# Rotary attention and two MLPs in one program: the first phase's side work given out in steps, SP and GpSimd in source order

## The chip, the cores and the metric

One core of one Trainium2 chip runs the whole program. The metric is device microseconds of one execution. TensorE is called PE here, VectorE DVE, ScalarE ACT, GpSimd POOL and SyncE SP; a load of PE's weights is PEld.

## The reference

```python
# q, k, v: (4, 8, 576, 64); x: (2304, 512); both MLPs 512 -> 2048 -> 512
q_rot, k_rot = rotate(q), rotate(k)          # rotary position embedding
scores = q_rot @ k_rot.T / sqrt(64)
attn = exp(scores - max(scores)); attn = attn / (sum(attn) + 1e-9)
x = (attn @ v), heads side by side           # (2304, 512)
h = x @ moe_w_in                             # first MLP
g = where(h >= 1, h, where(h <= -1, 0, (h + 1)**2 / 4))
x = g @ moe_w_out
h = x @ moe2_w_in                            # second MLP
g = s * relu(h)**2 + b
return g @ moe2_w_out
```

The first MLP's weights arrive as float64, everything else as float32.

## The kernel before

Every float32 operand of a product is split into a high part that PE multiplies in one pass and a low part, the rest; a product is then three passes (high by high, high by low, low by high), in the scores by stacking both parts over the 128 partitions.

**The first phase** is attention, with a part of the first MLP beside it. There are 16 pairs of heads (4 batches of 4 pairs). A pair has 9 units (`UNITS`), each 128 rows of scores against 576 keys, so there are 144 units. For unit n the loop at the end of the phase calls, in the order "qltaf":

- q: `qk`: 4 matmuls of 288 columns (8 in the third unit of a pair) into `sc`; on DVE the row maximum `nm` (L301); on ACT the exponential `p` (L304), with its row sums.
- l: `do_load`: the side work for the next pair (below), and every 4th or 5th unit `convert`.
- t: `tmain` and `trem` of unit n-2: PE transposes `p` into `tp` and `tr`, ACT copies the high part (`pth`, `ptr`), DVE subtracts for the low part (`ptl`).
- a: `av` of unit n-4, after every second unit: the product with v, and its sum `u` on DVE; after a pair's last unit `finish_pair` scales `u` and stores it to the DRAM array `xd` with three DMAs.
- f: `run_fill`: pieces of the first MLP on finished batches (`beside`): 12 matmuls into `h` or `y` per piece.

The side work for the next pair is the rotation and its splits: POOL multiplies q by the table, 4 instructions, and adds the halves, 2; ACT makes the high part `qin`, DVE the low part (L245). For k POOL makes the low part too (`rope_pair`, L234 to L252). Then SP stores the parts into the stacks `qs`, `kh` and `kz` with 10 DMAs (`stack`). v is split by ACT and POOL (`vs`). `convert` turns one half of a 128-row slice of float64 weights into its two float32 parts: a load `wraw`, ACT L124, DVE L125 to L128, ACT L129, POOL 4 instructions on L87 (`wm` twice, `w` twice). There are 16 such halves in the first phase. `split_x` loads a piece of `xd` as `xs` in four DMAs and splits it on ACT (`xh`) and POOL (`xl`).

**What sets the order.** The program is written once; a scheduler then walks it with a timeline of its own and decides each engine's order of instructions, and with that the order in which SP issues DMAs. `tc.issue_after(ins)` only says that an instruction must stand behind `ins` on its engine. Every engine then works through its list strictly in order, and waits on semaphores.

**The later phases** (L570 on, `stage`) do the rest of both MLPs, with PE's order that of the source. Their text is the same in both kernels.

Of the kernel before, what the change touches and what calls it, by code (L numbers as in the profile page):

```python
# [23 lines left out]
P = 128  # L24
# [5 lines left out]
WB = 1  # L30
# [12 lines left out]
LEAD = 4  # L43
# [8 lines left out]
CF = None  # L52
# [9 lines left out]
def kernel(ctx, tc, qq, kk, vv, tab, ww1, ww2, s, b, out):  # L62
# [37 lines left out]
    class Slice:  # L100
# [5 lines left out]
        def half(self, stage, bufs):  # L106
            if self.made == 0:
# [3 lines left out]
            raw = stage.tile([P, HW], self.ww.dtype, tag="wraw", name="wraw", bufs=RB)  # L111
            nc.sync.dma_start(out=raw, in_=self.ww[self.f, :, k:k + HW])
            hi, lo = self.w[:, 0, k:k + HW], self.w[:, 1, k:k + HW]
            if not wide:
                split(hi, lo, raw, nc.scalar, nc.gpsimd)
                return


            top = raw.bitcast(F32).rearrange("p (n t) -> p n t", t=2)[:, :, 1]
            low = raw.bitcast(U16).rearrange("p (n t) -> p n t", t=4)[:, :, 1]  # L120
            a = stage.tile([P, HW], F32, tag="wa", name="wa", bufs=bufs)
            m = stage.tile([P, HW], F32, tag="wm", name="wm", bufs=bufs)
            au, mu = a.bitcast(U32), m.bitcast(U32)
            nc.scalar.activation(a, top, AF.Copy, scale=2.0 ** -112)  # L124
            nc.vector.tensor_scalar(out=mu, in0=au, scalar1=3, scalar2=None, op0=ALU.logical_shift_left)  # L125
            nc.vector.scalar_tensor_tensor(out=mu, in0=au, scalar=0x80000000, in1=mu, op0=ALU.bitwise_and, op1=ALU.bitwise_or)  # L126
            nc.vector.tensor_scalar(out=au, in0=mu, scalar1=0xFF800000, scalar2=None, op0=ALU.bitwise_and)  # L127
            nc.vector.scalar_tensor_tensor(out=a, in0=low, scalar=2.0 ** -36, in1=a, op0=ALU.mult, op1=ALU.mult)  # L128
            nc.scalar.copy(hi, m)  # L129
            pool_tt(out=m, in0=m, in1=hi, op=ALU.subtract)  # L130
            pool_tt(out=lo, in0=m, in1=a, op=ALU.add)

    chains = {}

    def accumulate(out_ps, terms, chain=None):

        n = len(terms)
        with ExitStack() as st:
            if chain in chains:
                st.enter_context(tc.issue_after(chains[chain]))  # L140
            for i, (l, r) in enumerate(terms):
                m = nc.tensor.matmul(out_ps, l, r, start=(i == 0), stop=(i == n - 1))  # L142
        if chain is not None:
            chains[chain] = m.ins
# [62 lines left out]

    WHOLE = [slice(0, S)]
# [24 lines left out]

    def rope_pair(i, nm, eng, lo_eng, pieces=WHOLE):  # L234

        t = qk_in.pop((nm, i))
        hi, lo = t[:, 0, :].bitcast(F32R), t[:, 1, :].bitcast(F32R)
        for c in pieces:
            tt = pool_tt if eng is nc.gpsimd else nc.vector.tensor_tensor
            tt(out=t[:, :, c], in0=t[:, :, c], in1=tab_sb[:, :, c], op=ALU.mult)  # L240
            r = t[:, 1, c]
            tt(out=r, in0=t[:, 0, c], in1=r, op=ALU.add)
# [3 lines left out]
            else:  # L246
                nc.scalar.copy(hi[:, c], r)
                pool_tt(out=lo[:, c], in0=r, in1=t[:, 0, c], op=ALU.subtract)
        parts_t[nm, i] = t
        if i > 0:  # L250
            stack(i, nm, 0)
            stack(i, nm, 1)  # L252

    def stack(i, nm, j):
        t = parts_t[nm, i][j * D:(j + 1) * D]
        if nm == "q":
            st = stacks["q", i, j] = qs_t[j][i % 2]
# [114 lines left out]

    def finish_pair(i, e, eb):

        bb, hp = divmod(i, NP)
        u = u_t.pop(i)
        rm = bank("rm")
        for t in range(4):
# [297 lines left out]
```

## Time and profile before

| | |
|---|---|
| Median of 3 runs | 1205.93 us (1204.47 to 1206.97) |
| Profiled execution: its own time | 1205.45 us |
| Profiled execution: span of its instructions | 1203.6 us |
| PE, DVE, ACT, POOL busy, share of the span | 92%, 66%, 50%, 51% |
| Mean granted clock of PE | 0.98 of full speed |
| First unit's exponential; last unit's | 20.1 us; 480.9 us |

The shares are means over stages that have different limits. The first phase ends shortly after 480.9 us; behind it PE is nearly full. The profile's parts of use here are the busy time by stretch (one row for a piece of the span), the waits (engine and line that waited, for whom, us in total, times, longest) and the instructions in order of time, where a bracket gives the idle time ahead of an instruction and what ended it.

### The profile page before, as it was taken

The numbers are of one execution on the slowest core, as the hardware profiler recorded it, in microseconds if no ns is written. First come the engines' busy times: TensorE is split into PE (matmuls) and PEld (weight loads), VectorE is DVE, ScalarE is ACT, GpSimd is POOL, SyncE is SP. The second block draws the span as 40 slices with busy tenths as digits, with TensorE's granted clock in tenths as the row PEclk, the third lists the DMA queues.
The fourth block names the chain that finished last, engine by engine and source line by source line (L and its number), as shares of the span: only waits on it lengthen the run. The fifth ranks groups of instructions, "written<-read, shape, count | busy, mean of one in ns | idle before, by whom it ended". The sixth has DMA issues, their size and how long they took to land.

```text
span 1203.6 us, 19127 instructions
## 1 busy us (share of the span) xinstructions
PE 1109.6 (92%) x6628; PEld 1030.7 (86%) x6628; DVE 792.4 (66%) x1363; ACT 604.5 (50%) x1315; POOL 608.5 (51%) x778
## 2 busy tenths in 40 slices
PE   2887788897999999999999899999999999999998
PEld 2676678786989999999999899989888889988887
DVE  4777798897688777677766768677853333434443
ACT  3776677775767676545444434343433233222221
POOL 6878787878445310466688897567541101111000
PEclk9898899998999999999999999999999999999999
DMA  8666656556344420343334454443421101312220
GB/s 227 197 170 194 186 161 186 160 169 180 107 130 139 109 70 31 110 127 118 115 122 137 149 173 133 143 132 102 131 65 63 32 33 63 94 32 68 68 62 34
DMA packets 75840, 142.09 MB, mean 118 GB/s; under 512 B 12000, under 2 KB 49376, under 8 KB 75744
## 3 DMA queue, kind: packets, MB, share of 16 engines
q1 hardware_dynamic: 75744, 140.88, 39.9%
q8 instruction: 52, 0.85, 0.3%
q14 instruction: 44, 0.36, 0.1%
HBM read 90.70 MB, written 26.54 MB: 97 GB/s over the span
## 4 chain that ended last, share of the span: by engine, by line
PE 48%; DVE 16%; POOL 14%; DMA 9%; issue 7%; ACT 6%; SPq 1%; POOLq 0%; ACTq 0%; DVEq 0%
PE hps L142 15%; PE yps L589 5%; PE yps L591 5%; PE yps L590 5%; POOL w L87 5%; POOL wm L87 4%; PE sc L142 4%; PE av L142 3%; PE y L142 3%; PE h L142 3%; DMA xs<-xd 3%; POOL xl L87 3%; PE tp L317 3%; DVE wm L126 2%; DVE nm L301 2%
## 5 line engine op out<-in xcount | busy, mean ns | idle before, releaser
L142 PE MATMUL hps<-xh,w 128*128 128x464 f32 (+5 forms) x1216 | 345.4, 349 | 3.6 <-POOL w L87 2.5
L87 POOL TENSOR_TENSOR xl<-xs,xh 128x232 fp32r<-128x232 f32 (+5 forms) x168 | 131.5, 807 | 256.5 <-ACT xh L91 256.3
L142 PEld LDWEIGHTS hps<-xh,w 128*128 128x128 f32 x1216 | 222.4, 189 | 19.2 <-POOL w L87 2.8
L589 PE MATMUL yps<-gh,w 128*128 128x464 f32 (+5 forms) x608 | 213.8, 352 | 6.9 <-ACT yo L596 5.6
L590 PE MATMUL yps<-gl,w 128*128 128x464 f32 (+5 forms) x608 | 213.1, 351 | 3.2 <-DVE gl L95 3.2
L591 PE MATMUL yps<-gh,w 128*128 128x464 f32 (+5 forms) x608 | 212.6, 350 | 0.0
L142 PE MATMUL hps<-xl,w 128*128 128x464 f32 (+5 forms) x608 | 211.9, 349 | 0.0
L87 POOL TENSOR_TENSOR wm<-wm,w 128x256 f32<-128x256 f32 x128 | 116.1, 927 | 126.0 <-DVE wa L127 66.8
L142 PE MATMUL sc<-kh,qs 128*128 128x288 f32 x320 | 103.5, 338 | 50.4 <-ACT p L304 32.3
L174 DVE TENSOR_TENSOR ar<-ar,hps 128x464 f32<-128x464 f32 (+1 forms) x80 | 50.6, 632 | 132.7 <-ACT ar L173 132.7
L301 DVE TENSOR_REDUCE nm<-sc 128x1 f32<-128x576 f32 x144 | 108.2, 752 | 40.0 <-PE sc L142 38.4
L589 PEld LDWEIGHTS yps<-gh,w 128*128 128x128 f32 x608 | 114.8, 189 | 17.8 <-ACT yo L596 8.2
L590 PEld LDWEIGHTS yps<-gl,w 128*128 128x128 f32 x608 | 114.8, 189 | 12.0 <-DVE gl L95 4.6
L591 PEld LDWEIGHTS yps<-gh,w 128*128 128x128 f32 x608 | 114.9, 189 | 7.5
L142 PEld LDWEIGHTS hps<-xl,w 128*128 128x128 f32 x608 | 114.5, 188 | 7.6
L304 ACT ACTIVATE p<-sc,nm 128x576 f32<-128x576 f32 x144 | 106.9, 745 | 19.3 <-DVE nm L301 15.3
L142 PEld LDWEIGHTS sc<-kh,qs 128*128 128x128 f32 x320 | 64.7, 202 | 59.4 <-ACT p L304 39.6
L323 DVE TENSOR_TENSOR ptl<-tp,pth 128x512 fp32r<-128x512 f32 x134 | 90.5, 683 | 25.9 <-ACT pth L319 24.7
L173 ACT ACTIVATE ar<-hps 128x464 f32<-128x464 f32 (+1 forms) x80 | 44.2, 553 | 124.8 <-PE hps L142 124.5
L87 POOL TENSOR_TENSOR w<-wm,wa 128x256 fp32r<-128x256 f32 x128 | 99.7, 797 | 0.0
L319 ACT CAST pth<-tp 128x512 fp32r<-128x512 f32 x134 | 77.7, 585 | 39.5 <-PE tp L317 38.9
L142 PE MATMUL sc<-kz,qs 128*128 128x288 f32 x320 | 95.1, 311 | 0.0
(85 smaller groups left out, 2289.5 us busy)
## 6 DMA issues: line engine op xcount, KB each, us to landing
wraw<-in_ww SPq DMA_DIRECT2D x64, 512.0 KB, 4.1
kh<-kin SPq DMA_DIRECT2D x64, 144.0 KB, 3.4
qs<-qin SPq DMA_DIRECT2D x64, 144.0 KB, 2.6
qin<-in_q SPq DMA_DIRECT2D x15, 576.0 KB, 5.3
kin<-in_k SPq DMA_DIRECT2D x15, 576.0 KB, 3.8
xs<-y1d SPq DMA_DIRECT2D x32, 232.0 KB, 2.5
xs<-xd SPq DMA_DIRECT2D x40, 144.0 KB, 2.6
yd<-ys SPq DMA_DIRECT2D x40, 144.0 KB, 2.1
```

Source lines behind the costliest of these rows:

```text
L87: nc.gpsimd.tensor_tensor(out=out[c], in0=in0[c], in1=in1[c], op=op)
L142: m = nc.tensor.matmul(out_ps, l, r, start=(i == 0), stop=(i == n - 1))
L173: nc.scalar.activation(r, ps, AF.Relu)
L174: nc.vector.tensor_tensor(out=r, in0=r, in1=ps, op=ALU.mult)
L301: nc.vector.tensor_reduce(out=nm, in_=sc[:, :, :288], axis=AX.XY, op=ALU.max, negate=True)
L304: nc.scalar.activation(p, sc[:, :, :288], AF.Exp, bias=nm, scale=1.0, accum_out=sums_t[i][:, col:col + 1])
L317: nc.tensor.transpose(v[:, c, :], p_t[i, k][:, c * P:(c + 1) * P], ident)
L319: nc.scalar.copy(hi, v)
L323: nc.vector.tensor_tensor(out=lo, in0=v, in1=hi, op=ALU.subtract)
L589: nc.tensor.matmul(acc, wh, gh, start=f == 0, stop=False)
L590: nc.tensor.matmul(acc, wh, gl, start=False, stop=False)
L591: nc.tensor.matmul(acc, wl, gh, start=False, stop=last)
```

## The change

**Source order for two engines.** The loop of the first phase runs inside `tc.manual_schedule` for SP and POOL: in it their instructions stand in the order in which the program writes them. DVE, ACT and PE are still ordered by the scheduler.

**Steps given out later.** `put(n, fn)` keeps a step for unit n; `run_later(n)` runs the kept steps directly behind unit n's scores, maximum and exponential. `behind` places each step's DVE and ACT instructions behind the newest maximum and exponential (`anchors`). For pair i+1 rotation and stores are spread over units 1 to 7 of pair i, a conversion's steps over 4 units from the one after it is called, the load of `xd` 3 units behind a finished batch and its splits 2 and 3 units behind the load, the store of `u` one unit and the store of `y` two units behind their sources. The whole rotation of one tile is now one step where the first pair's is done in halves.

**x in one load.** `split_x` loads all four pieces with one DMA, into the tile of the low parts, which is subtracted in place.

**Stores by kind.** The first pair's stores stand kh, kz, qs for both heads; before they alternated by head.

**Fill.** `run_fill` carries at most one unit of unused budget, and stops when the x it needs is not due yet; `LEAD` is gone.

The diff, cut to its core:

```diff
+        def steps(self, stage, bufs):
+            ...
+            return [load, bias, shift, high, rest, low_part]
...
+    anchors, later = {}, {}
+    def put(n, fn, *args):
+        later.setdefault(n, []).append((fn, args))
+    def behind(fn, *args):
+        with ExitStack() as st:
+            for ins in anchors.values():
+                st.enter_context(tc.issue_after(ins))
+            fn(*args)
+    def run_later(n):
+        for fn, args in later.pop(n, []):
+            behind(fn, *args)
...
-        nc.vector.tensor_reduce(out=nm, in_=sc[:, :, :288], axis=AX.XY, op=ALU.max, negate=True)
+        anchors["DVE"] = nc.vector.tensor_reduce(out=nm, in_=sc[:, :, :288], axis=AX.XY, op=ALU.max, negate=True).ins
...
-        nc.scalar.activation(p, sc[:, :, :288], AF.Exp, bias=nm, scale=1.0, accum_out=sums_t[i][:, col:col + 1])
+        anchors["ACT"] = nc.scalar.activation(p, sc[:, :, :288], AF.Exp, bias=nm, scale=1.0, accum_out=sums_t[i][:, col:col + 1]).ins
...
+        put(now + 1, u_store, i, u)
...
-    def split_x(c):
-        xh = m1.tile([P, KD, N1], F32R, tag="xh", name="xh")
-        xl = m1.tile([P, KD, N1], F32R, tag="xl", name="xl")
-        for k in range(KD):
-            xs = m2.tile([P, N1], F32, tag="xs", name="xs", bufs=1)
-            nc.sync.dma_start(out=xs, in_=xd[k, :, c * N1:(c + 1) * N1])
-            split(xh[:, k, :], xl[:, k, :], xs, nc.scalar, nc.gpsimd)
-        return xh, xl
+    def x_load(c):
+        x_t["h"] = m1.tile([P, KD, N1], F32R, tag="xh", name="xh")
+        x_t["l"] = m1.tile([P, KD, N1], F32R, tag="xl", name="xl")
+        nc.sync.dma_start(out=x_t["l"].bitcast(F32), in_=xd[:, :, c * N1:(c + 1) * N1].rearrange("k p n -> p k n"))
+    def x_split(k):
+        l = x_t["l"][:, k, :]
+        split(x_t["h"][:, k, :], l, l.bitcast(F32), nc.scalar, nc.gpsimd)
+    def split_x(c, n):
+        put(n, x_load, c)
+        for k in range(KD):
+            put(n + 2 + k // 2, x_split, k)
+        return n + 4
...
-                nc.sync.dma_start(out=yd[gi, d, :, c * N1:(c + 1) * N1], in_=y)
+                put(now + 2, y_store, gi, d, c, y)
...
+    def convert_turns(sl, n):
+        steps = sl.steps(wst, WB)
+        steps[0]()
+        for dn, step in zip((2, 2, 3, 3, 4), steps[1:]):
+            put(n + dn, step)
...
-                elif k == 1:
-                    rope_pair(i + 1, "q", nc.gpsimd, nc.vector)
-                elif k == 3:
-                    rope_pair(i + 1, "k", nc.gpsimd, nc.gpsimd)
-                elif k == 5:
-                    load_v(i + 1)
-                elif k == 7:
-                    v_pair(i + 1)
+                    for dn, fn, nm in ((1, rope_mult, "q"), (2, rope_add, "q"), (3, rope_hi, "q"), (4, rope_lo, "q"),
+                                       (3, rope_mult, "k"), (4, rope_add, "k"), (5, rope_hi, "k"), (6, rope_lo, "k")):
+                        put(n + dn, fn, i + 1, nm)
+                    put(n + 4, load_v, i + 1)
+                    put(n + 5, stack_q, i + 1)
+                    put(n + 6, stack_k, i + 1)
+                    put(n + 7, stack_z, i + 1)
+                    put(n + 6, v_hi, i + 1)
+                    put(n + 7, v_lo, i + 1)
...
-            convert()
+            convert(n + 1)
...
+        done = min(done, 1.0)
         done += budget
...
+    with tc.manual_schedule(engines={mybir.EngineType.SP, mybir.EngineType.Pool}):
+        while now < len(units) + LA or fill or later:
...
+                for o in ORDER:
+                    acts[o](now) if now < len(units) + LA or o == "f" else None
+                    if o == "q":
+                        run_later(now)
```

How the built programs stand, at three places. First ACT, from the transposed copies of the first pair on (`pth`; L319 before, L375 now; `wa` and `w` are a conversion's two ACT steps, `p` is a unit's exponential). Before, from its row 8, then the change, from its row 6:

```order
L319 COPY pth_211<-tp 128x4x128
L271 CAST vs<-vin 128x5x2x64
L304 ACTIVATE p,sums<-sc,nm 128x576
L124 ACTIVATE wa<-wraw 128x512
L319 COPY pth_211<-tp 128x4x128
L129 CAST w<-wm 128x512
L319 COPY pth_211<-tp 128x4x128
L304 ACTIVATE p,sums<-sc,nm 128x576
```

```order
L375 COPY pth_207<-tp 128x4x128 x3
L360 ACTIVATE p,sums<-sc,nm 128x576
L289 ACTIVATE qin<-qin 128x576
L389 COPY ptr_208<-tr 64x384
L360 ACTIVATE p,sums<-sc,nm 128x576
L375 CAST pth_274<-tp 128x4x128
L360 ACTIVATE p,sums<-sc,nm 128x576
L291 CAST kin<-kin 128x576
```

The conversion is gone from pair 0; its first ACT step now stands behind the exponential of pair 1's third unit. Up to the end of pair 4 ACT begins 6 conversions before and 8 now.

Second ACT where the first x is split (`xh`; L91 before, L89 now). Before, pair 1's seventh unit and on; then the change, the end of pair 4:

```order
L304 ACTIVATE p,sums<-sc,nm 128x576
L353 COPY u<-av 64x320
L91 CAST xh<-xs 128x288
L319 COPY pth_469<-tp 128x4x128
L304 ACTIVATE p,sums<-sc,nm 128x576
```

```order
L375 CAST pth_3202<-tp 128x4x128 x2
L389 CAST ptr_3204<-tr 64x256
L89 CAST xh<-xl 128x288 x2
L417 COPY u<-av 64x320
L360 ACTIVATE p,sums<-sc,nm 128x576
L89 CAST xh<-xl 128x288 x2
```

Before, one quarter of the first x is split after each of the pairs 0 to 3; now all four quarters are, a batch's four pairs being stored.

Third POOL, about pair 2 (multiplications by `tab_sb` and additions are the rotation for the next pair, `wm` and `w` a conversion, `eb` the sums of the pair before). Before, from row 43, then the change, from row 48:

```order
L87 TENSOR_TENSOR kin<-kin,tab_sb 128x2x144 x4
L87 TENSOR_TENSOR w<-wm,wa 128x256 x2
L87 TENSOR_TENSOR xl<-xs,xh 128x288
L87 TENSOR_TENSOR kin<-kin 128x288 x2
L87 TENSOR_TENSOR qin<-qin,tab_sb 128x2x144 x4
L370 COPY eb<-sume 128x512
L87 TENSOR_TENSOR kin<-kin,tab_sb 128x2x144 x4
L87 TENSOR_TENSOR qin<-qin 128x288
```

```order
L85 TENSOR_TENSOR qin<-qin,tab_sb 128x2x144 x4
L426 COPY eb<-sume 128x512
L85 TENSOR_TENSOR wm<-wm,w 128x256 x2
L85 TENSOR_TENSOR w<-wm,wa 128x256 x2
L85 TENSOR_TENSOR qin<-qin 128x288 x2
L85 TENSOR_TENSOR kin<-kin,tab_sb 128x2x144 x4
L85 TENSOR_TENSOR kin<-kin 128x288 x4
```

Before, the multiplications of k stand ahead of `eb`, up to a pair early, and the parts of a rotation are mixed with conversions. Now q, k and their low parts follow `eb` in one run, with a conversion's four instructions between, and k's low part (the last two of the x4) comes last.

On PE the counts of product matmuls per pair move by a few; behind the last pair's transposes 72 `h` and `y` matmuls are left, 48 before. On SP the last four `y` stores now stand behind eleven `xs` loads of the next phase, where five such loads stood ahead of the first of them.

## Rows read from the trace of the kernel before

**Rows 1.** Busy time by stretch; columns: PE, PEld, DVE, ACT, POOL, PEclk, DMA share, GB/s.
```profile
45.10:146.60 101.50, 79.53 (x510) 67.93 (x507) 80.55 (x137) 74.03 (x171) 80.37 (x100) 0.92 0.66 181
146.60:303.20 156.60, 131.19 (x917) 121.80 (x918) 137.62 (x246) 109.95 (x259) 125.53 (x155) 0.95 0.62 175
303.20:480.90 177.70, 172.22 (x1313) 168.36 (x1312) 135.69 (x256) 124.62 (x303) 56.88 (x75) 0.99 0.34 96
...
515.00:1203.60 688.60, 671.27 (x3529) 620.80 (x3527) 395.07 (x651) 258.16 (x500) 299.53 (x380) 1.00 0.31 95
200.00:250.00 50.00, 42.21 (x302) 39.50 (x302) 45.25 (x82) 36.37 (x88) 39.09 (x48) 0.97 0.64 181
```

**Rows 2.** Waits of PE and ACT, 45.1 to 303.2 us.
```profile
PE sc L142 <- ACT p L304: 23.7, 17, 4.7
...
ACT xh L91 <- DMA xs<-xd: 21.2, 11, 5.7
```

**Rows 3.** SP in order of time, 104 to 110 us.
```profile
104.29 0.42 SPq L386 DMA_DIRECT2D xd<-u  x1
...
109.91 0.33 SPq L396 DMA_DIRECT2D xs<-xd  x1
```

**Rows 4.** ACT in order of time, 106 to 114 us.
```profile
106.23 0.42 ACT L361 COPY u<-av 64x320 f32<-64x320 f32 x1
112.38 0.43 ACT L91 CAST xh<-xs 128x288 fp32r<-128x288 f32 x1 [5.72 <-DMA xs<-xd]
```

**Rows 5.** ACT in order of time, pair 0's first conversion.
```profile
24.93 0.74 ACT L304 ACTIVATE p<-sc,nm 128x576 f32<-128x576 f32 x1
...
27.79 0.66 ACT L124 ACTIVATE wa<-wraw 128x512 f32<-128x512 f32 x1 [2.02 <-DMA wraw<-in_ww]
...
30.66 0.62 ACT L129 CAST w<-wm 128x512 fp32r<-128x512 f32 x1 [1.73 <-DVE wm L126]
...
31.66 0.74 ACT L304 ACTIVATE p<-sc,nm 128x576 f32<-128x576 f32 x1
```

**Rows 6.** DVE groups, 45.1 to 303.2 us: busy us, mean ns.
```profile
L128 DVE SCALAR_TENSOR_TENSOR wa<-wraw,wa 128x512 f32<-128x512 uint16 x16 | 13.8, 862 | 0.2
L126 DVE SCALAR_TENSOR_TENSOR wm<-wa,wm 128x512 uint32<-128x512 uint32 x16 | 13.5, 845 | 0.2
...
L125 DVE TENSOR_SCALAR wm<-wa 128x512 uint32<-128x512 uint32 x16 | 11.6, 726 | 3.6 <-ACT wa L124 3.6
...
L127 DVE TENSOR_SCALAR wa<-wm 128x512 uint32<-128x512 uint32 x16 | 8.2, 510 | 0.2
```

**Rows 7.** POOL groups, 45.1 to 303.2 us.
```profile
L87 POOL TENSOR_TENSOR kin<-kin,tab_sb 128x288 f32<-128x288 f32 x40 | 35.4, 914 | 6.2 <-DMA kin<-in_k 3.8 <-issue 2.4
L87 POOL TENSOR_TENSOR wm<-wm,w 128x256 f32<-128x256 f32 x30 | 25.4, 865 | 19.7 <-DVE sume L368 6.9 <-DVE wa L127 6.8 <-ACT pth L319 3.6
L87 POOL TENSOR_TENSOR w<-wm,wa 128x256 fp32r<-128x256 f32 x30 | 21.6, 738 | 0.0
L87 POOL TENSOR_TENSOR kin<-kin 128x288 f32<-128x288 f32 x21 | 17.7, 854 | 0.0
```

**Rows 8.** ACT in order of time: exponentials of pair 2's first and fifth, pair 3's first unit.
```profile
69.92 0.75 ACT L304 ACTIVATE p<-sc,nm 128x576 f32<-128x576 f32 x1
...
80.53 0.74 ACT L304 ACTIVATE p<-sc,nm 128x576 f32<-128x576 f32 x1
...
90.88 0.74 ACT L304 ACTIVATE p<-sc,nm 128x576 f32<-128x576 f32 x1
```

**Rows 9.** DMA issues: count, KB each, median us to landing.
```profile
kz<-kin SPq DMA_DIRECT2D x32, 144.0 KB, 3.1
```

**Rows 10.** The conversion's tile wa, 45.1 to 303.2 us: ns shortest/median/longest.
```profile
L125 DVE TENSOR_SCALAR wm<-wa x16: 404/820/1029, 48.6 to 295.3; 128x512 uint32<-128x512 uint32 x16
```

**Rows 11.** The y copies' tile, 303.2 to 481 us: DMA to landing.
```profile
DMA to landing us min/median/max: 1.7/2.0/3.6
```

**Rows 12.** ACT in order of time behind the last pair.
```profile
497.05 0.43 ACT L91 CAST xh<-xs 128x288 fp32r<-128x288 f32 x1 [3.79 <-DMA xs<-xd]
```

More of the change, by code (lines that the diff above doesn't have):

```diff
@@ L106, in half @@
         def half(self, stage, bufs):
+            for step in self.steps(stage, bufs):
+                step()
+        def steps(self, stage, bufs):
             if self.made == 0:
@@ L133 @@
-    chains = {}
-    def accumulate(out_ps, terms, chain=None):
-        n = len(terms)
[L138 to L144, printed above, removed]
+                return [load, lambda: split(hi, lo, t["raw"], nc.scalar, nc.gpsimd)] + [lambda: None] * 4
@@ new lines, in high, with rest, low_part @@
+            def high():
+                nc.scalar.copy(hi, t["m"])
+            def rest():
+                low = t["raw"].bitcast(U16).rearrange("p (n t) -> p n t", t=4)[:, :, 1]
+                a = t["a"]
+                nc.vector.tensor_scalar(out=a.bitcast(U32), in0=t["m"].bitcast(U32), scalar1=0xFF800000, scalar2=None, op0=ALU.bitwise_and)
+                nc.vector.scalar_tensor_tensor(out=a, in0=low, scalar=2.0 ** -36, in1=a, op0=ALU.mult, op1=ALU.mult)
+            def low_part():
+                m = t["m"]
+                pool_tt(out=m, in0=m, in1=hi, op=ALU.subtract)
+                pool_tt(out=lo, in0=m, in1=t["a"], op=ALU.add)
@@ L433 @@
     load_v(0)
-    rope_pair(0, "k", nc.vector, nc.gpsimd, HALVES)
-    rope_pair(0, "q", nc.vector, nc.vector, HALVES)
-    for j in range(2):
-        stack(0, "k", j)
-        first = stack(0, "q", j)
-    v_pair(0)
+    rope_first("k")
+    rope_first("q")
+    stack_k(0)
+    stack_z(0)
+    first = stack_q(0)
+    v_hi(0)
+    v_lo(0)
     nc.sync.dma_start(out=s_sb, in_=s.to_broadcast([P, 1]))
@@ L461, in run_fill @@
             try:
-                done -= next(fill[0])
+                cost = next(fill[0])
+                if cost is None:
+                    break
+                done -= cost
             except StopIteration:
@@ L517 @@
     acts = {"q": do_qk, "l": do_load, "t": do_t, "a": do_av, "f": do_fill}
-    for n in range(len(units) + LA):
-        with ExitStack() as st:
-            if n < 36:
-                st.enter_context(tc.issue_after(first))
-            for o in ORDER:
-                acts[o](n)
-    while fill:
-        run_fill(1.0)
+    now = 0
+    with tc.manual_schedule(engines={mybir.EngineType.SP, mybir.EngineType.Pool}):
+        while now < len(units) + LA or fill or later:
+            with ExitStack() as st:
+                if now < 36:
+                    st.enter_context(tc.issue_after(first))
+                for o in ORDER:
+                    acts[o](now) if now < len(units) + LA or o == "f" else None
+                    if o == "q":
+                        run_later(now)
+            now += 1
     pa.close()
```

141 lines of the change are left out of this document (83 added, 58 removed).

## The prediction, made before the changed kernel ran

> **What bounds the kernel now.** I read the busy time by stretch first, cut at the first exponentials of pairs 0, 1, 5 and 10 at the last unit and where the next phase begins. The reader should see three regimes [rows 1]. From 515 us on PE is nearly full: 671.27 of 688.60 us. The change doesn't touch that code, so nothing is to be had there. From 303.2 to 480.9 us PE is busy 172.22 of 177.70 us; what the change could win is 5.5 us at the most. The room is ahead of that. In pairs 1 to 4 (101.5 us) no engine is full: PE 79.53, DVE 80.55, POOL 80.37, ACT 74.03. In pairs 5 to 9 (156.6 us) DVE has 137.62, PE 131.19. So 283 us, the 25 of pair 0 with them (20.1 to 45.1), go to engines that wait for each other, and the question is what they wait for.
>
> The waits say it next. PE waits 23.7 us for exponentials, to reuse its score buffers [rows 2]. So the pace is that of maximum and exponential, and I ask what stands in their way on ACT and DVE. On ACT the largest wait for something outside the units is `xh` for its load: 21.2 us in 11 waits [rows 2]. In order of time one reads like this: SP issues the store of `u` at 104.29 us, and the load `xs` of the same data only at 109.91 [rows 3]; ACT, done at 106.65, stands until 112.38, 5.72 us, with copies and exponentials queued behind `xh` [rows 4]. A second kind is a conversion ahead of its data. In pair 0 ACT waits 2.02 us for `wraw` and 1.73 us for DVE inside one conversion, and two neighbouring exponentials are 6.7 us apart, 24.93 to 31.66 [rows 5].
>
> **The change part by part.** The sum is made on the profiled execution, 1205.45 us (its span 1203.6); the median of the runs is 1205.93, 0.5 us above.
>
> *Pair 0.* No conversion is left in it. Its four DVE steps, two ACT steps and the load wait go. The gap of 6.7 us falls to a common unit: pair 2 took (90.88 - 69.92)/9 = 2.3 us for each [rows 8]. That is 4.4 us. Against it the second qs store of the first head now stands behind two more kh and one more kz; SP takes about 0.5 us for an issue (0.42 for the one in rows 3), and the first scores wait for it: 0.5 us. **Minus 4.** Bounds: 0, if pair 0 then waits for the next pair's k instead; 5.
>
> *Pairs 1 to 4.* The three `xs` waits in here go, since the load now follows the store by two units and the splits follow the load by two more; two more conversions come in (8 begun by the end of pair 4, 6 before). A conversion costs DVE 862 + 845 + 726 + 510 ns = 2.94 us [rows 6], POOL 2 x 865 + 2 x 738 = 3.2 us [rows 7]. DVE's work is then 80.55 + 5.9 = 86.4 us, POOL's 80.37 + 6.4 = 86.8. The fullest long stretch of the trace while POOL is also busy has DVE at 45.25 of 50 us, 90% [rows 1]. At that packing the stretch would take 96 us, 5.5 less. But here there is no product work to fill with and the rotation's own chain (first rival) is close behind, so I take **minus 2**. Bounds: minus 10 (DVE at 94%) and plus 7 (the rival).
>
> *Pairs 5 to 9.* Two conversions fewer: DVE's work 137.62 - 5.9 = 131.7 us; the `h` matmuls and their steps are as many as before. The other eight `xs` waits go. One DMA issue and its landing take the place of four; two units lie ahead of the first split, and I let them cover it: a unit here is 156.6/45 = 3.5 us, two are 7, and one quarter's load took 2.5 us from issue to use [rows 3, 4]. If the fourfold load took more than 7 us, ACT would wait again. At 90.5% of DVE the stretch takes 145.5 us: **minus 11**. Bounds: 0 and minus 18 (95%).
>
> *Pairs 10 to 15.* PE is full, so gains end here. A new cost: `y` has two buffers, and its store now comes two units after the copy. The third copy of a piece waits for the first one's store, which lands 2.0 us after its issue [rows 11], behind the qs, kh and kz stores on SP. ACT has 53 us free in this stretch, so most of it hides. **Plus 4**, from 0 to 12 (1 us on ACT for half of the 24 copies if it hides behind nothing).
>
> *End of the phase.* 72 matmuls instead of 48 are left behind the last transposes; the last `h` need ACT and DVE in turn, while ACT splits the next phase's x in the same list and already waits 3.79 us for a load there [rows 12]. Before, PE had cover for it. **Plus 3**, 0 to 6.
>
> The store of `u` one unit later, v's split, the merged tiles: nothing, as the first is read two units later and POOL's and ACT's counts stay the same. SP in source order: each of its waits is about one unit behind the step it waits for; what could be late is kz, the rival below.
>
> Sum: 1205.45 - 4 - 2 - 11 + 4 + 3 = **1195 us**.
>
> **The rivals.** *POOL's list becomes the bound (slower).* Now k's rotation stands behind `eb` and a conversion in strict order. Take pair 2's first exponential as zero. The conversion's POOL part waits for its last DVE step, which is placed behind the maximum of a later unit, in pair 2 of its fifth, whose exponential comes at 10.6 us [rows 8]. Add that DVE step 0.86 [rows 6], POOL's part 3.2, k's multiplication 4 x 0.914 = 3.7, addition 1.7, high part on ACT about 0.7 (as long as the exponentials, 0.74), low part 1.7, the landing of kz 3.1 [rows 9], scores and maximum some 1.5: the next pair's first exponential at 27.2 us. A pair took 101.5/4 = 25.4. So pairs 1 to 4 lose 7.3 us; if pairs 5 to 9 gain nothing for the same reason, the time is 1205.45 - 4 + 7.3 + 7 = 1216. It decides once kz lands later than two exponentials ahead of its pair. For it: POOL is already 79 to 80% busy there [rows 1]. Against: POOL runs ahead whenever its data are there, only some pairs have the conversion ahead of k, and at 2.3 us a unit, the mean of the same pair, the fifth exponential would come at 9.2 us, which takes 1.4 us off the chain.
>
> *DVE and POOL can't be packed closer (no change).* L125 takes 404 ns at best and 1029 at worst on the same shape [rows 10]. Something stretches DVE's SBUF-to-SBUF work here. If it and POOL excluded each other fully, the bound on pairs 1 to 9 would be POOL's 80.37 + 125.53 = 205.9 us [rows 1] plus DVE's conversions, 13.8 + 13.5 + 11.6 + 8.2 = 47.1 us [rows 6]. That is 253 us of 258.1, so 5 us to win at most; I take 3, and the time is 1205.45 - 4 - 3 + 7 = 1205. Against: if they stretch each other, these durations contain their own waits, and the true bound lies lower. The Trainium skill, "SBUF — State Buffer", section "Who interferes with whom", says just this: a DVE instruction with two SBUF inputs, or in a two-port mode, and a GpSimd instruction that reads SBUF lock each other out for a whole instruction. The trace agrees in kind, with the 404 and 1029 ns above; by that rule the time would be this rival's.
>
> *DVE packs to 95% and the new costs hide.* Minus 10 and minus 18 in the two stretches, minus 4 at the start: 1174 with nothing given back, some 1181 with both late costs.
>
> **How the numbers follow.** Forecast 0.56, POOL bound 0.22, no closer packing 0.13, close packing 0.09. About 0.2% (2.4 us) is what a measurement of this kernel can tell from no change. The forecast's own range, 1187 to 1204, holds a small part within that. Faster 0.56 x 0.95 + 0.09 = 0.62; within 0.2%: the rest of the forecast, 0.03, and 0.10 of the third case: 0.13; slower 0.22 + 0.03 = 0.25. The range goes from 1178, inside the close packing, to 1216, the price of the POOL bound.
>
> **What would show it.** Right: no `xh` waits of several us on ACT in pairs 1 to 9; no 6.7 us between exponentials of pair 0; the first exponential of pair 10 some 17 us earlier than 303.2, DVE about 90% busy in pairs 5 to 9; PE's wait for exponentials well below 23.7 us. For the first rival: PE waits for kz at the first scores of pairs 2 to 5, and ACT's high part of k waits for POOL. For the second: longer means on POOL and DVE than in [rows 6, 7], the stretch as long as before. The late costs would be ACT's `ys` waiting for the store of `y`, and a gap of PE near the last pair's end. I am wrong if pairs 1 to 9 are not shorter, or if the time lies outside 1178 to 1216.

## The result, and the profile of the changed kernel

The change makes the kernel slower: 1214.8 us (median of 6 runs, 1212.77 to 1220.86) against 1205.0 us for the kernel before on the same chip; the ratio is 1.0084, its 95% interval 1.006 to 1.0108. The forecast was faster, 1195 us. The profiled execution of the changed kernel took 1214.13 us (span 1212.4), 8.7 us more than before.

Busy time by stretch of the changed kernel, cut at the same exponentials as [rows 1], with pair 0 ahead; columns as there:

```profile
20.80:40.70 19.90, 17.64 (x102) 14.98 (x101) 9.43 (x15) 14.56 (x35) 7.97 (x11) 1.00 0.49 131
40.70:153.20 112.50, 84.74 (x515) 70.60 (x514) 88.32 (x153) 75.53 (x173) 80.74 (x102) 0.91 0.59 170
153.20:302.30 149.10, 127.85 (x911) 118.67 (x911) 128.25 (x230) 106.73 (x254) 110.38 (x139) 0.97 0.55 162
302.30:482.90 180.60, 171.33 (x1294) 164.85 (x1293) 138.62 (x259) 123.60 (x306) 80.26 (x105) 1.00 0.41 119
```

Pair 0 is 5.1 us shorter (19.9 against 25.0) and pairs 5 to 9 are 7.5 us shorter (149.1 against 156.6). But pairs 1 to 4 are 11.0 us longer (112.5 against 101.5), pairs 10 to 15 2.9 us longer, and from the last exponential to the end there are 729.5 us, 6.7 more than before (722.8).

The waits of PE and ACT in the changed kernel, pairs 1 to 9 (engine, line, whom for: us in total, times, longest):

```profile
ACT p L360 <- DVE nm L357: 13.9, 13, 3.2
PE sc L156 <- ACT p L360: 11.3, 13, 2.1
PE sc L156 <- DMA kz<-kin: 7.9, 5, 2.8
ACT xh L89 <- DMA xl<-xd: 5.6, 3, 3.6
```

The wait that the change is about fell: ACT's `xh` stands 5.6 us for its load where it stood 21.2 (3.6 of the 5.6 are one wait, for the first load of x at the end of pair 4), and PE's wait for exponentials fell from 23.7 to 11.3 us [rows 2]. In its place PE now waits 7.9 us for `kz`, k's low part, for which nothing waited in these pairs before. Where that stands is seen at the end of pair 3, on SP and then on PE, in order of time (start, duration; in brackets the idle time ahead and what ended it):

```profile
112.35 0.60 SPq L316 DMA_DIRECT2D kh<-kin  x1
112.99 0.58 SPq L119 DMA_DIRECT2D wraw<-in_ww  x1
113.67 1.10 SPq L321 DMA_DIRECT2D kz<-kin  x2
...
117.28 0.31 PE L156 MATMUL av<-ptr,vs 128*128 128x320 f32 x1
119.55 0.40 PE L156 MATMUL sc<-kz,qs 128*128 128x288 f32 x1 [1.96 <-DMA kz<-kin]
```

SP issues a load of weights, `wraw`, and 0.7 us later the two kz stores. PE runs dry at 117.59 us and gets kz at 119.55; the next pair's first exponential follows at 121.2, 7.5 us after the issue. Before, kz was issued 7 to 45 us ahead of its pair (pairs 1 to 10), as POOL and SP ran up to a pair ahead.

The load ahead of kz is waited for as well. ACT and DVE at the same place, and ACT at the end of pair 4:

```profile
118.64 0.66 ACT L129 ACTIVATE wa<-wraw 128x512 f32<-128x512 f32 x1 [2.30 <-DMA wraw<-in_ww]
119.33 0.43 DVE L134 TENSOR_SCALAR wm<-wa 128x512 uint32<-128x512 uint32 x1 [2.07 <-ACT wa L129]
120.32 0.76 DVE L357 TENSOR_REDUCE nm<-sc 128x1 f32<-128x576 f32 x1
...
149.79 0.76 ACT L89 CAST xh<-xl 128x288 fp32r<-128x288 f32 x2 [3.61 <-DMA xl<-xd]
```

At the end of pair 3 the maximum `nm` stands on DVE behind the conversion's step and one that follows ACT's next copy, so with kz there earlier it could hardly have started before 120.3 us. At the end of pair 4 PE stands 2.78 us for kz, until 150.68, and ACT for x until 149.79; the next pair's first exponential, at 153.24, stands behind both.

### The profile page after: what moved, and what is told of

Read it like the earlier page. It is cut to its first block, busy times and chain, and to the rows that moved or that the text cites. A ratio compares the mean times of both kernels' runs of the same rounds, so it can differ in the third digit from the quotient of the medians.

```text
span 1212.4 us, 19014 instructions
## 1 busy us (share of the span) xinstructions
PE 1113.7 (92%) x6628; PEld 1030.9 (85%) x6628; DVE 790.4 (65%) x1363; ACT 602.1 (50%) x1315; POOL 602.5 (50%) x778
## 4 chain that ended last, share of the span: by engine, by line
PE 47%; POOL 15%; DVE 15%; issue 8%; ACT 7%; DMA 6%; SPq 2%; POOLq 0%; ACTq 0%; DVEq 0%
PE hps L156 15%; PE yps L678 5%; PE yps L680 5%; PE yps L679 5%; POOL w L85 4%; POOL wm L85 4%; PE sc L156 4%; PE y L156 4%; PE h L156 3%; DMA kz<-kin 3%; PE av L156 3%; POOL xl L85 3%; DVE wm L135 2%; DVE nm L357 2%; PE tp L373 2%
## 5 line engine op out<-in xcount | busy, mean ns | idle before, releaser
L85 POOL TENSOR_TENSOR xl<-xs,xh 128x232 fp32r<-128x232 f32 (+5 forms) x140 | 106.0, 787 | 216.9 <-ACT xh L89 216.9
L156 PE MATMUL sc<-kh,qs 128*128 128x288 f32 x320 | 102.8, 336 | 37.9 <-DMA qs<-qin 18.7
L678 PEld LDWEIGHTS yps<-gh,w 128*128 128x128 f32 x608 | 115.1, 189 | 18.7 <-ACT yo L685 8.1
L360 ACT ACTIVATE p<-sc,nm 128x576 f32<-128x576 f32 x144 | 107.3, 746 | 27.5 <-DVE nm L357 24.6
L375 ACT CAST pth<-tp 128x512 fp32r<-128x512 f32 x134 | 77.8, 586 | 43.3 <-PE tp L373 42.2
```

The lines of the kernel that those rows point to most:

```text
L85: nc.gpsimd.tensor_tensor(out=out[c], in0=in0[c], in1=in1[c], op=op)
L360: anchors["ACT"] = nc.scalar.activation(p, sc[:, :, :288], AF.Exp, bias=nm, scale=1.0, accum_out=sums_t[i][:, col:col + 1]).ins
L375: nc.scalar.copy(hi, v)
L678: nc.tensor.matmul(acc, wh, gh, start=f == 0, stop=False)
```

## The experiments

Each ratio is to runs of the kernel before on the same chip, with its 95% interval; the stretches come from one profiled execution each, cut as above. "kz" is the median time from issue to landing of the kz stores between 40 and 160 us. How far a stretch repeats is seen on two kernels with the same program through pair 11: the change and e11 took 112.5 and 111.1 us for pairs 1 to 4, but 149.1 and 156.2 for pairs 5 to 9. The profiled execution of e7 is the fastest of its six, 1186.7 us against a median of 1192.7; e16, the same program through pair 13, took 99.3 and 142.6 us for these two stretches.

| run | ratio | pairs 1-4 | 5-9 | 10-15 | behind | kz |
|---|---|---|---|---|---|---|
| before | 1 | 101.5 | 156.6 | 177.7 | 722.8 | 4.6 |
| change | 1.0084 | 112.5 | 149.1 | 180.5 | 729.5 | 4.3 |
| e1 k two units earlier | 1.0414 (1.0392-1.0436) | 121.6 | 172.1 | 189.8 | 729.0 | 3.0 |
| e2 stores at once | 1.0215 (1.0188-1.0241) | 116.6 | 164.1 | 179.1 | 731.2 | 4.5 |
| e3 change, free order | 1.0125 (1.0104-1.0147) | 107.3 | 161.5 | 177.7 | 732.2 | 6.2 |
| e4 before, source order | 1.1355 (1.1332-1.1377) | 155.7 | 244.9 | 202.0 | 723.1 | 2.6 |
| e5 k one unit earlier | 1.0089 (1.0069-1.0108) | 110.2 | 152.2 | 179.3 | 731.8 | 2.7 |
| e6 before + x | 0.9975 (0.9957-0.9994) | 94.8 | 159.3 | 173.3 | 732.3 | 5.6 |
| e7 before + rotation | 0.9904 (0.9882-0.9927) | 96.1 | 142.4 | 179.6 | 722.5 | 3.0 |
| e8 before + x + conversions | 1.0019 (0.9998-1.0041) | 90.7 | 167.2 | 173.1 | 731.9 | 5.2 |
| e9 before + rotation + x | 1.0067 (1.0043-1.0092) | 106.4 | 150.5 | 176.4 | 733.1 | 5.2 |
| e10 as e9, + conversions | 1.0107 (1.0081-1.0133) | 103.7 | 160.9 | 181.1 | 730.4 | 5.2 |
| e11 change, more fill | 1.0075 (1.0046-1.0104) | 111.1 | 156.2 | 184.7 | 722.6 | 3.9 |
| e12 as e9, more fill | 1.0027 (1.001-1.0045) | 107.4 | 147.6 | 183.3 | 722.4 | 5.2 |
| e13 change, loads clear of kz | 1.0063 (1.0039-1.0087) | 105.7 | 156.2 | 182.5 | 730.4 | 2.7 |
| e14 change, two loads in the way | 1.0156 (1.0132-1.018) | 119.5 | 150.1 | 181.5 | 730.3 | 6.1 |
| e15 as e13, more fill | 1.0053 (1.0034-1.0072) | 103.1 | 155.4 | 185.0 | 722.2 | 2.7 |
| e16 as e7, more fill | 0.9923 (0.9906-0.9939) | 99.3 | 142.6 | 181.7 | 729.3 | 3.4 |
| e17 as e9, no cap | 1.0149 (1.0107-1.0192) | 103.7 | 163.9 | 186.8 | 716.0 | 4.7 |
| e18 as e13, cap early | 1.0082 (1.005-1.0115) | 103.8 | 159.4 | 188.1 | 726.4 | 2.7 |

### e1 and e5: k earlier

```diff
-(3, rope_mult, "k"), (4, rope_add, "k"), (5, rope_hi, "k"), (6, rope_lo, "k")
+(1, rope_mult, "k"), (2, rope_add, "k"), (3, rope_hi, "k"), (4, rope_lo, "k")
```

In e1 with stack_k at n + 4 and stack_z at n + 5; in e5 all these numbers are one larger.

> The changed kernel with the four rotation steps of k and its kh and kz stores two units earlier; all else as in the change. Theory A (kz comes just in time, so the next pair's first scores wait): kz is issued some 5 us earlier in each pair, PE's wait for kz in pairs 1 to 9 falls from 9.6 us to under 3, pairs 1 to 4 from 112.6 us to 103 to 108, and the time to 1204 to 1209. Theory B (DVE and POOL stretch each other and cannot be packed closer): the kz waits go, but others take their place, pairs 1 to 4 stay at 110 to 115 us, the time at 1212 to 1217. Theory C (the stores of y and the late fill at the phase's end): 1212 to 1217 as well, with the milestones behind 480 us unchanged relative to the last exponential.

> The changed kernel with the rotation steps of k and its kh and kz stores one unit earlier, so that its multiplication still stands behind eb in POOL's list (two units earlier it stood ahead of eb, and the third unit of a pair then waited for eb). Theory A (kz just in time): PE's wait for kz in pairs 1 to 9 falls from 9.6 us to under 4, pairs 1 to 4 from 112.6 us to 106 to 110, the time to 1206 to 1211. Theory E (in a strict list every place moved ahead makes something else late: conversion, eb, ACT's list): kz's waits shrink, others grow by as much, 1213 to 1225.

Two units earlier PE's wait for kz is down to 0.5 us, and the kernel is 4% slower. The waits of e1, 40 to 334 us:

```profile
PE rm L434 <- POOL eb L426: 43.0, 9, 12.4
DVE u L435 <- PE rm L434: 23.9, 5, 10.4
```

k's multiplication now stands ahead of `eb`, the finished pair's sums, in POOL's strict list, and PE stands for `eb` up to 12.4 us at a time. One unit earlier, PE waits 12.7 us for `eb` in pairs 1 to 9 and 5.7 for kz, and the time is that of the change, as theory E had it. Theory A in its simple form (kz is late, so move it) fell: the place that k leaves is taken from something that is needed as much.

### e2, e3, e4: stores at once, and the order

```diff
-put(now + 2, y_store, gi, d, c, y)
+y_store(gi, d, c, y)
-put(now + 1, u_store, i, u)
+u_store(i, u)
```

> The changed kernel with the stores of u and y written where their data are made, not one and two units later; SP still in source order. Theory C (delayed stores hold back the end of the phase): ACT's ys no longer waits for the store of y, the time from the last exponential to the end falls from 729.5 us towards 723, the time to 1207 to 1210. Theory A: the end gains at most 2 us, and SP, which now stands before each store until its data are there, issues kz no earlier or later: 1212 to 1219.

> The changed kernel without the source order: steps and their places behind maxima and exponentials kept, SP and POOL ordered by the scheduler again. Theory D (source order on SP and POOL is what makes kz late): POOL and SP run ahead, kz is issued 7 us or more ahead of its pair, pairs 1 to 4 take 101 to 105 us, the time is 1202 to 1207. Theory A in its narrow form (the steps are late, since ACT's high part of k stands behind the exponential of the sixth unit whatever the order on SP and POOL): kz is no earlier than in the change, pairs 1 to 4 take 109 to 114 us, 1211 to 1217.

> The kernel before with its first phase in source order on SP and POOL, and nothing else of the change: rotation written at units 1 and 3, stores right behind it. Theory D (source order is what costs): SP stands before each store and load until its data are there, POOL behind conversions; pairs 1 to 4 take 108 us or more, the time is 1212 or more. Theory A in its narrow form (the late steps cost, not the order): k is rotated from the fourth unit of a pair on, kz is in time, pairs 1 to 4 take 100 to 106 us, the time is 1202 to 1209.

e3 takes the line `with tc.manual_schedule(...)` out of the change; e4 puts it around the loop of the kernel before. Theory D fell in e3 and came out in e4. In e3 kz is issued 8 to 11 us ahead at the ends of pairs 1 to 4, as theory D wanted, and pairs 1 to 4 take 107.3 us; but pairs 5 to 9 take 161.5, and without source order the steps are no faster (1.0125 against 1.0084). So in the change source order is not what costs. Without the steps it costs 13.6%: e4 waits, 41 to 442 us,

```profile
PE rm L379 <- POOL eb L370: 123.3, 9, 28.7
POOL wm L87 <- DVE wa L127: 66.7, 6, 15.6
```

show POOL standing at a conversion with `eb` queued behind it. Steps placed units later are what makes such an order bearable. e2 says the same of SP: with the stores at once the ratio rises by 1.3%, most of it in pairs 5 to 9, so the delays of u and y help; the end does not get shorter (731.2 us), and theory C fell.

### e6 to e10: the parts one by one, SP and POOL free

Each is the kernel before with parts of the change's diff, the order left to the scheduler. The part on x (its fill rule with it), the rotation with its stores, and the conversions, by their calls:

```diff
-x = split_x(work[0][0])
+ready = split_x(work[0][0], now + 3)
...
-rope_pair(i + 1, "q", nc.gpsimd, nc.vector)
+for dn, fn, nm in ((1, rope_mult, "q"), (2, rope_add, "q"), (3, rope_hi, "q"), (4, rope_lo, "q"),
...
-convert()
+convert(n + 1)
```

e6 has the first, e7 the second, e8 the first and third, e9 the first and second, e10 all three.

> The kernel before with only the part on x: one load of all four pieces three units after a finished batch, splits two and three units later behind the newest maximum and exponential, the fill waiting for it; rotation, conversions, stores and SP's and POOL's free order as before. Theory A (the x part gains, the late rotation costs): no waits of ACT's xh for a load in pairs 1 to 9, pairs 5 to 9 at 145 to 150 us, the time 1194 to 1201. Rival (the x waits only covered other waits): 1203 to 1209.

> The kernel before with only the rotation, v's split and their stores given out as the change does it, behind maxima and exponentials; x, conversions, y and u stores and SP's and POOL's free order as before. Theory A (late rotation is the cost): PE waits for kz 8 us or more in pairs 1 to 9, pairs 1 to 4 at 107 to 113 us, the time 1210 to 1220. Rival (the rotation steps are harmless, conversions in POOL's list make them late): kz's waits under 3 us, 1202 to 1208.

> The kernel before with the part on x and with the conversions in steps, rotation and stores as before, free order. Theory A: as with x alone, and pair 0 free of its conversion: 1191 to 1199. Rival (conversion steps behind maxima hold up POOL's rotation): kz waits of several us, pairs 1 to 4 at 107 us or more, 1205 to 1215.

> The kernel before with the rotation given out in steps and the part on x (its fill rule with it), conversions, u and y stores and the free order as before. Theory F (rotation steps gain, and only together with the conversion's steps do they cost): pairs 1 to 4 at 90 to 98 us, last exponential at 450 to 463 us, the stretch from it to the end at 730 us or more as with x alone, so 1182 to 1194. Rival (any two parts get in each other's way): pairs 1 to 4 above 101 us, 1203 to 1215.

> As the run with rotation and x, and the conversions in steps too; only the delayed stores of u and y and the source order are then missing from the change. Theory F: pairs 1 to 4 at 104 to 112 us with PE waiting for kz 10 us or more, 1213 to 1224, as the change with SP and POOL free (1221). Rival G (the delayed stores of u and y cost, not the conversions): pairs 1 to 4 at 90 to 99 us, 1184 to 1198.

x alone (e6) gains 0.25%, less than expected: `xh` waits only 0.5 us for its load in pairs 1 to 9, but pairs 5 to 9 take 159.3 us, not 145 to 150. The conversions in steps add 0.4% both times (e8 to e6, e10 to e9; the latter two intervals overlap). They lengthen pairs 5 to 9 (167.2 and 160.9 us); pairs 1 to 4 get no longer with them (90.7 and 103.7 us). Theory F fell with e9.

e7 turned the picture round. The rotation in steps, which I had as the cost, gains 1% alone and makes the fastest kernel of all. Its stretches (pairs 1 to 4, 5 to 9) and two of its waits, pairs 1 to 9:

```profile
44.40:140.50 96.10, 78.32 (x510) 64.70 (x507) 83.89 (x147) 74.05 (x172) 80.13 (x104) 0.96 0.62 180
140.50:282.90 142.40, 125.74 (x914) 117.32 (x915) 127.61 (x227) 105.14 (x252) 107.71 (x133) 0.99 0.59 172
...
ACT xh L91 <- DMA xs<-xd: 4.8, 5, 2.1
PE sc L142 <- DMA kz<-kin: 3.8, 4, 1.5
```

With x untouched, four loads and all, the `xh` waits are down from 21.2 us to 4.8. And kz is just as late as in the change: issued 4.7 to 7.4 us ahead of its pair (pairs 1 to 9; 4.2 to 11.0 in the change). So lateness alone is not the cost, and x in one load is not needed for the gain. With rotation and x together (e9) pairs 1 to 4 take 10 us more than with rotation alone (8 us from e16 to e12). The landing times of kz, 40 to 160 us, in e7, e9 and e6, in this order:

```profile
DMA to landing us min/median/max: 2.5/3.0/5.1
...
DMA to landing us min/median/max: 3.0/5.2/6.6
...
DMA to landing us min/median/max: 2.7/5.6/6.0
```

At the median kz lands 2 us later in e9 than in e7. But only at the end of pair 4 does a load of x stand ahead of it, by 3.6 us (the first kz store lands in 4.9 us, in e7 in 2.5). At the end of pair 3 it is the load of a later pair's k, 576 KB, 0.5 us ahead (5.5 us, in e7 2.5), and at the end of pair 1 one of weights, which e7 has there too (6.5 and 5.1 us). In e6, where POOL runs up to a pair ahead, kz lands as late, but from pair 2 on it is issued 9 to 49 us ahead, PE never waits for it between 40 and 160 us, and pairs 1 to 4 take 94.8 us. So it seems to take both: a late kz, and something that holds up its landing.

### e13 and e14: loads out of kz's way, and into it

In e13 a conversion's load of weights that would fall in the sixth to eighth unit of a pair is issued in the fifth, its other steps unmoved, and the first load of x stands behind kz; in e14 two loads (units 17 and 25) are issued in units 15 and 24.

```diff
-if n > 5 and n % (CA if n < 36 else CB) == 0:
-    convert(n + 1)
+for c in CONV:
+    if early(c + 1) == n + 1:
+        convert(n + 1, c + 1)
```

Here `CONV` lists the old units, the second argument sets the other steps, and `early(n)` is `n - n % 9 + 4 if n % 9 in (5, 6, 7) else n` in e13 and `{17: 15, 25: 24}.get(n, n)` in e14.

> The changed kernel in which a conversion's load of weights that would be issued in the sixth to eighth unit of a pair is issued in the fifth, all its other steps where they were, and the first load of x is issued two units later, behind kz. Theory J (a large load issued just ahead of kz delays kz's landing): the time from the issue of kz to the next pair's first exponential falls from 7.5 to about 5 us at the end of pair 3 and from 11.0 to 5 to 6 at the end of pair 4; pairs 1 to 4 at 103 to 108 us, the time at 1205 to 1211. Rival K (what makes these pairs long is the order on ACT, DVE and POOL, not the loads): the times from issue to exponential fall little or the pairs stay at 110 to 114, 1212 to 1218.

> The changed kernel in which two loads of weights (of the third and the fifth conversion) are issued two and one units earlier, between the stores of kh and kz of pairs 2 and 3, where none stands in the change; all other steps where they were. Theory J: from issue of kz to the first exponential 7 us or more for pairs 2 and 3, 4.2 and 4.9 in the change; pairs 1 to 4 longer by 4 to 8 us, 1218 to 1223. Rival K: no difference beyond 1 us in these pairs, 1212 to 1217.

e14, end of pair 2, on SP, PE and DVE; here the change had `kh` and `kz` side by side:

```profile
91.81 0.59 SPq L316 DMA_DIRECT2D kh<-kin  x1
92.45 0.59 SPq L119 DMA_DIRECT2D wraw<-in_ww  x1
93.14 1.10 SPq L321 DMA_DIRECT2D kz<-kin  x2
...
99.09 0.40 PE L156 MATMUL sc<-kz,qs 128*128 128x288 f32 x1 [3.17 <-DMA kz<-kin]
...
99.80 1.42 DVE L357 TENSOR_REDUCE nm<-sc 128x1 f32<-128x576 f32 x2 [2.89 <-PE sc L156]
```

and kz's landing between 40 and 160 us in e13, in the change and in e14:

```profile
DMA to landing us min/median/max: 2.6/2.7/2.7
...
DMA to landing us min/median/max: 2.6/4.3/8.4
...
DMA to landing us min/median/max: 5.7/6.1/7.4
```

Boundary by boundary (ends of pairs 1, 2, 3, 4) the landing takes 2.6, 2.7, 6.0 and 7.8 us in the change, 2.6, 2.7, 2.7, 2.7 in e13 and 5.9, 6.1, 6.1, 7.1 in e14: with each load of 512 KB put ahead of kz it takes 3.3 to 3.4 us more, and with each taken away it comes back. From issue of kz to the first exponential pairs 2 and 3 go from 4.2 and 4.9 us to 9.2 and 7.5 (e14), pairs 4 and 5 from 7.5 and 11.0 to 4.5 and 4.4 (e13). Pairs 1 to 4 follow: 105.7 us in e13 (103.1 and 103.8 in e15 and e18, which place the loads alike), 112.5 in the change, 119.5 in e14. So the place of these loads sets the length of this stretch, as theory J had it. The Trainium skill, "DMA: Bandwidth & Descriptors", section "Queues, rings and completion order", gives a reason: a DMA engine takes one queue's descriptors in ring order, and the semaphore is raised only after that engine's earlier writes. The trace agrees with it, 6.0 against 2.7 us.

How much of this is kz alone is not shown. Of the ends in e14 that of pair 2, above, shows kz's landing by itself, and there it costs 2.6 us. At the end of pair 1 PE also works in another order than in the change: ten products with v, 3.05 us, stand ahead of the first product with kz, not behind it, and PE goes from them to kz without a gap. And e13 takes away more than the load ahead of kz. ACT's waits for `wraw` and `xl`, 3.4 and 3.6 us in pairs 1 to 4 of the change, go with it, and some work on the first x falls behind pair 4 (DVE is busy 85.4 us in the stretch, 88.3 in the change). In e18 kz lands within 3.6 us, and still 7.5 us pass at the end of pair 3 from its issue to the exponential.

The whole time followed up (1.0156) but only a little down: 1.0063 has an interval that overlaps the change's. e13, e15 and e18 take 155 to 159 us for pairs 5 to 9, where the first x, and with it the fill, comes two units later; whether that is why was not tried, and e11, without it, took 156.2.

### e11, e12, e15 to e18: the end of the phase

```diff
-run_fill(0.55 if n < 18 * NP + LA else 0.95)
+run_fill(0.55 if n < 18 * NP + LA else 0.95 if n < 108 else 1.05)
```

This is e11, e12 and e15; in e16 the 1.05 starts at unit 126. e17 drops `done = min(done, 1.0)`; e18 keeps it up to unit 90 only.

> The changed kernel with a budget of 1.05 pieces a unit from the thirteenth pair on, not 0.95, so that 60 product matmuls are left behind the last transposes, 12 of them h, not 72 with 24 h behind the last product with v. Theory H (the new fill rule leaves h matmuls behind the last pair, whose chain over DVE and ACT nothing covers): the stretch from the last exponential to the end falls from 729.5 to 721 to 725 us, of which part may come back before it, 1207 to 1211. Rival (the late y stores hold the end): 1213 to 1217.

> The run with rotation and x, with that budget of 1.05 from the thirteenth pair on. Theory F and H together: 1176 to 1187, that is 6 us below the run with rotation and x. Rival (pairs 10 to 15 are full, what is filled earlier lengthens them by as much): the same time as that run.

> The kernel of the run with the loads clear of kz, with a budget of 1.05 pieces a unit from the thirteenth pair on. Theory J with H: 2 to 4 us below that run, 1202 to 1208, with the stretch from the last exponential to the end at 722 to 724 us. Rival: as that run, what is won at the end being lost ahead of it.

> The kernel before with only the rotation in steps (ratio 0.990 alone), and a budget of 1.05 pieces a unit in the last two pairs, so that no h matmul is left behind the last product with v. Theory H: 1 to 3 us below rotation alone, a ratio of 0.987 to 0.990 to the kernel before. Rival (pairs 14 and 15 are full): the ratio of rotation alone, 0.990 to 0.993. If the gain of rotation alone hangs on the chip it ran on, a ratio over 0.995.

> The run with rotation and x (ratio 1.007), with unused fill budget kept, not capped at one unit, so that no product matmul of the first MLP's part is left behind the last pair. Theory H (the cap is what x brought along): the stretch from the last exponential to the end at 722 us or less, not 733, a ratio of 0.990 to 0.998. Theory J (the large load of x ahead of kz and the later fill lengthen pairs 4 to 9): the end is shorter, but pairs 1 to 9 stay at 250 us or more and the ratio above 0.999.

> The changed kernel with the loads clear of kz (ratio 1.0063), and the cap on unused budget only up to the tenth pair, so that 42 y matmuls and no h are left behind the last transposes. Theory H: the stretch from the last exponential to the end at 720 to 724 us and a ratio of 0.998 to 1.003. Rival (pairs 10 to 15 are full): 1.004 to 1.008.

Every kernel with the new fill rule unaltered has 729 to 733 us behind the last exponential. In the change PE stands there, and the granted clock falls (PE in order of time, then busy time by stretch):

```profile
509.86 0.29 PE L156 MATMUL y<-gh,w 128*128 128x288 f32 x1
511.97 0.40 PE L678 MATMUL yps<-gh,w 128*128 128x288 f32 x1 [1.83 <-ACT ys L494]
...
502.00:507.00 5.00, 5.00 (x40) 5.00 (x39) 2.11 (x6) 2.03 (x5) 2.60 (x4) 1.00 0.49 126
507.00:512.00 5.00, 3.17 (x25) 2.94 (x23) 3.30 (x8) 4.00 (x10) 1.25 (x2) 1.00 0.24 80
512.00:517.00 5.00, 5.00 (x26) 5.00 (x27) 1.14 (x3) 1.29 (x2) 1.75 (x3) 0.66 0.54 166
```

The 24 more matmuls at 5.00/40 = 0.125 us make 3.0 us, the gap 1.8, and 5 us at a granted clock of 0.66 cost 1.7: together 6.5 of the 6.7 us. With the larger budget this part falls to 722 us (e11, e12, e15), as theory H had it; but pairs 10 to 15 grow by 4.2, 6.9 and 2.5 us. What is left over is seen once: from e9 to e12 the ratio falls from 1.0067 to 1.0027, with intervals that just touch. From e13 to e15 and from the change to e11 nothing can be told. e17 and e16 bound it. Without any cap (e17) the end is 716 us, but the fill piles up in pairs 5 and 9 (38.5 and 42.8 us long) and the kernel is slower still. With no h left behind the last pair (e16) PE reaches the next phase before its x is split, the end takes 729.3 us, and the ratio is no better than e7's. e16, PE and busy time by stretch:

```profile
486.04 0.40 PE L142 MATMUL hps<-xh,w 128*128 128x288 f32 x1 [2.15 <-ACT xh L91]
...
488.30:493.30 5.00, 4.64 (x20) 4.38 (x19) 3.69 (x6) 2.45 (x6) 2.96 (x4) 0.50 0.59 168
```

So the fill rule is at most a part of why e9 is slower than e7: e12, without the long end, is still at 1.0027. e18 shortened the end to 726.4 us only and did not beat the kernel before. The versions that beat both are e7, e16 and, by 0.25%, e6.

## Why the prediction was wrong

**Pairs 1 to 4: the step that failed.** The forecast was minus 2, within minus 10 and plus 7; it came out at plus 11. Of the 18.7 us between the forecast's sum (minus 10) and the measured span (plus 8.7), 13 stand here. The step let DVE take two more conversions and be packed to 90%, less something for the rotation's chain. DVE's work came out nearly as forecast (88.3 us against 86.4), but DVE was busy 79% of the stretch: the waits for loads and stores that now come just in time were put at nothing. kz was taken for a matter of the first rival alone, whose price was plus 7.3 (its terms add up to 27.1 us, not 27.2, which makes it 6.8).

That rival named the right wait. That its time, 1216 us, is nearly the measured one is luck: it had pairs 5 to 9 unchanged and 7 us lost behind them, and measured are minus 7.5 and plus 9.6. Its reason was half of it. It put the lateness on POOL's list, with a conversion ahead of k, and took the landing at the median of 3.1 us [rows 9]. But e7 has the same lateness without conversion steps, and is fast. What I did not work out is that source order on SP also fixes which load stands just ahead of kz: at the ends of pairs 3 and 4 that is a load of weights, or of weights and x, the landing takes 6.0 and 7.8 us, and ACT stands for these loads itself. The order in which SP issues could be read ahead of the run; the page's median hid the range. Some 7 of the 11 us go when these loads are moved (e13), by kz's landing and the loads' own waits together; the runs don't part the two.

The other 4 us stay open. Pair 2 took 26.2 us against 21.0 before, and 26.5 in e13, with kz landing in 2.7 us. The number of conversions alone is not the reason: e7 begins nine by the end of pair 4, the change eight, and pairs 1 to 4 take 96.1 us in e7. Of the second rival, the locking of DVE and POOL, the sign did not come as a whole: the four DVE steps of a conversion took 2.54 us at the mean in pairs 1 to 9, 2.94 before. A small part shows in DVE's low part of q in pairs 1 to 4, in the change and in e7; the mean of the change is made of 1.2 to 1.4 us three times and 3.45 us once, in pair 4, with POOL's multiplications and additions beside it:

```profile
L297 DVE SCALAR_TENSOR_TENSOR qin<-qin 128x576 fp32r<-128x576 f32 x4 | 7.3, 1834 | 0.6 <-ACT qin L289 0.6
...
L284 DVE SCALAR_TENSOR_TENSOR qin<-qin 128x576 fp32r<-128x576 f32 x4 | 3.4, 838 | 0.0
```

**Pair 0: right.** Minus 4 was forecast; the first exponential of pair 1 comes at 40.7 instead of 45.1 us, 4.4 earlier. ACT's third and fourth exponentials, 6.7 us apart in [rows 5], now start at

```profile
24.81 0.74 ACT L360 ACTIVATE p<-sc,nm 128x576 f32<-128x576 f32 x1 [2.21 <-DVE nm L357]
...
28.75 0.75 ACT L360 ACTIVATE p<-sc,nm 128x576 f32<-128x576 f32 x1
```

They are 3.9 us apart, not the 2.3 forecast, so this gap gave 2.8 of the 4.4 us; where the rest was won was not looked into.

**Pairs 5 to 9: the mechanism right, the size uncertain.** Minus 11 was forecast, minus 7.5 measured; the same program in e11 took 156.2 us, minus 0.4. The `xh` waits did fall as forecast, from 7.4 to 2.0 us here (the trace of before has seven of them here and four in pairs 1 to 4, not eight and three). That two units cover the fourfold load held for the later loads, which landed in 4.1 to 5.0 us; the first, in pair 4, took 8.2. DVE was busy 86%, not 90.5. And e7 shows that they fall, and 14 us with them, by the rotation's steps alone.

**Pairs 10 to 15 and the end.** Plus 4 was forecast and 2.9 measured; ACT's `ys` did stand for the store of `y`, 4.0 us in two waits. For the end plus 3 was forecast, 0 to 6, and 6.7 measured. The extra matmuls alone make 3.0; the gap, which the forecast named among its signs, and the granted clock after it come on top.

**What stays open.** With the loads clear of kz the kernel is still 0.5 to 0.8% slower than before (e13, e15, e18), so they are not the whole reason. Rotation alone gives 0.990, x alone 0.9975, both 1.0067: together 1.9% worse than their product. In pairs 1 to 4 most of it stands between the issue of kz and the first exponential of pairs 2 to 5 (e9 loses 8.4 us there to e7, 7.3 of them by the landing of the first store). Why pairs 5 to 9 are 8 us longer is not settled. It is not a load of x ahead of kz: at the ends of pairs 5 and 9 that load has landed before kz is issued, and at the ends of pairs 7 and 8 the load ahead is one of weights.

## What to carry to other kernels

Before a transfer is made to come just in time, read what the same queue issues in the few microseconds ahead of it: a load of 512 KB there made two stores land 3.3 to 3.4 us later, and where the consumer was 9 us or more away (e6) PE never waited for them. See also whether that load is itself waited for. Try the parts of a change one by one: here the best part, alone, was worth 1%, and the whole was a loss. Shortening the last stretch by moving work ahead of it gains little when the stretch ahead is full.

## What the hardware showed unexpectedly

At the ends of pairs 1 to 4 of the change, e13 and e14 the two kz stores of 144 KB landed 2.6 to 2.7 us after their issue when no load stood just ahead of them, and 5.7 to 6.3 when a 512 KB load was issued 0.7 us ahead; with a load of weights and one of x ahead, 6.8 to 8.4. A gap of PE of 1.8 us was followed by a granted clock of 0.66 over the next 5 us, part of it at the lower of the two levels (1.2 of 2.4 GHz); in the kernel before the clock stayed at 1.00 there. In pairs 1 to 4 the mean granted clock was 0.96 in e7, 0.91 in the change and 0.86 in e14, but 0.90 in e13, which is 6.8 us shorter there than the change. DVE's low part of q took 0.75 us twice where POOL stood still (e7), and 1.2 to 3.45 us beside POOL's multiplications and additions (the change); but once in e7 it took 0.75 us beside a POOL addition too.
